# Experts' second layer: two of three row tiles by seven half-width products, accumulated in PSUM

## The chip, the core and the metric

The kernel runs on one core of one Trainium2 chip. The metric is the device time of one execution in microseconds (us); lower is better. A core has five engines that each run their own instructions in order and wait for each other through semaphores: TensorE (PE; its weight loads are listed apart as PEld), VectorE (DVE), ScalarE (ACT), GpSimd (POOL) and SyncE (SP, which only starts transfers here). PE takes its operands from SBUF and writes its sums into PSUM[...]; DVE and ACT read them from there.

## The reference, cut

An attention block (a gated linear recurrence with matrix memory) makes one row of 320 numbers for each of 3072 tokens. Then each token goes through one of 8 experts, chosen by a hash of its id:

```python
N, D, E, F = (3072, 320, 8, 1024)
# w1: (E, D, F), w2: (E, F, D), all float32
expert_idx = token_ids * np.int64(2654435761) % np.int64(E)
for e in range(E):
    mask = expert_idx == e
    xe = x[mask]
    h = np.maximum(xe @ w1[e], 0.0)
    out[mask] = h @ w2[e]
```

The change touches only `h @ w2[e]`.

## The kernel before

The attention block takes the first part of the run and stores the rows of x in memory. The experts follow, one after the other. Each handles 3 tiles of 128 of its tokens and up to 32 more (CAP = 416 columns); the remainders of four experts at a time share one tile (`rest`), and a loop at the end, empty for these inputs, takes what is still left over. `h` is kept transposed: for each of the FB = 8 blocks of F, 128 partitions of F by 416 tokens, so that a slice of it is the stationary operand (lhsT) of the second layer and a block of w2, 128 by 320, the moving one (rhs). [...] two banks of `tp`, four of `mh`, two of `zp`. The pool `xp` keeps two buffers of a tile unless `bufs` says otherwise.

```python
    def scatter(zp, idx, apart):
        zo = xp.tile([P, Dm], F32, name="zo", bufs=4)
        nc.scalar.copy(zo[:], zp[:])
        ins = nc.gpsimd.indirect_dma_start(
            out=out[:, :], out_offset=bass.IndirectOffsetOnAxis(ap=idx, axis=0),
            in_=zo[:], in_offset=None, bounds_check=N - 1, oob_is_err=False,
        )
        ins = getattr(ins, "ins", ins)
        if apart:
            tc.declare_no_dep(ins, group="rows_out", reason="disjoint rows")
            tc.add_to_no_dep_group("rows_out", ins)

# ... turn(): transposes of the rows into xT (PE), a 64-column pad copy on DVE, and the eviction of tp ...

    def layer1(w, xT, h, cols, between=lambda fp: None):

        w1t, w1c, _ = w
        for fp in range(FB // 2):
            hp = [mps.tile([P, CAP], F32, name="mh", bufs=4) for _ in range(2)]

            def halves(first):
                for i in range(2):
                    r = slice(i * P // 2, (i + 1) * P // 2)
                    nc.tensor.matmul(
                        hp[i][:, :cols], lhsT=w1c[r, fp, :], rhs=xT[r, 2, :cols], start=first, stop=not first,
                    )

            def whole(i, first):
                fb = 2 * fp + i
                for db in range(2):
                    nc.tensor.matmul(
                        hp[i][:, :cols], lhsT=w1t[:, db, fb * P : (fb + 1) * P], rhs=xT[:, db, :cols],
                        start=(first and db == 0), stop=(not first and db == 1),
                    )

            def out(i):
                if i == 0:
                    nc.vector.tensor_relu(h[:, 2 * fp, :cols], hp[i][:, :cols])
                else:
                    nc.scalar.activation(h[:, 2 * fp + 1, :cols], hp[i][:, :cols], AF.Relu)

            if fp % 2 == 0:
                for i in range(2):
                    whole(i, True)
                between(fp)
                halves(False)
                for i in range(2):
                    out(i)
            else:
                halves(True)
                for i in range(2):
                    whole(i, False)
                    out(i)
                between(fp)

    def layer2(w, h, n, idx, apart, between=lambda j: None):
        for j in range(n):
            zp = mps.tile([P, Dm], F32, name="zp")
            for fb in range(FB):
                nc.tensor.matmul(
                    zp[:], lhsT=h[:, fb, j * P : (j + 1) * P], rhs=w[2][:, fb, :],
                    start=(fb == 0), stop=(fb == FB - 1),
                )
            scatter(zp, idx(j), apart)
            between(j)

```

The loop over the experts; `fetch` gathers the rows of an expert on the GpSimd queue, `turns` gives the four pieces of work that transpose the next expert's rows, and layer 1 calls one of them in each of its four steps:

```python
# ...
        def rest(g):
            zp = mps.tile([P, Dm], F32, name="zp")
            for fb in range(FB):
                for i in range(EG):
                    nc.tensor.matmul(
                        zp[i * RM : (i + 1) * RM, :], lhsT=hrem[g][:, i, fb, :], rhs=W[g * EG + i][2][:, fb, :],
                        start=(fb == 0), stop=(fb == FB - 1),
                    )
            scatter(zp, cols_of(s_idx, NR + g)(0), True)

# ...
        for e in range(E):
            g, i = e // EG, e % EG
            if e + 2 < E:
                fetch(e + 2)
            h = xp.tile([P, FB, CAP], F32, name="h")
            if i == 0:
                hrem[g] = xp.tile([P, EG, FB, RM], F32, name="hrem")
            ahead = turns(e + 1) if e + 1 < E else []

            def one(_):
                if ahead:
                    ahead.pop(0)()
                for _ in range(3):
                    if third:
                        third.pop(0)(nc.scalar)

            def after(j):
                one(j)
                if j == 0 and i == EG - 1:
                    rest(g)

            layer1(W[e], xTs[e], h, CAP, one)
            nc.gpsimd.tensor_copy(hrem[g][:, i], h[:, :, NM:])
            layer2(W[e], h, NJ, cols_of(s_idx, e * NJ), True, after)
            if e + 3 < E:
                load_weights(e + 3)

```

Of the kernel before, what the change touches and what calls it, by code (L numbers as in the profile page):

```python
# [8 lines left out]
F32 = mybir.dt.float32  # L9
# [5 lines left out]
ALU = mybir.AluOpType  # L15
PSUM = bass.MemoryType.PSUM

P = 128
# [4 lines left out]
def kernel(  # L23
# [24 lines left out]
    nc = tc.nc  # L48
# [4 lines left out]
    Dm = H * D  # L53
    E, _, F = moe_w1.shape
    FB = F // P
# [10 lines left out]
    NJ = 3  # L66
# [17 lines left out]
    s_idx = consts.tile([P, NC], I32, name="s_idx")  # L84
    xe = consts.tile([1, NX + 1], I32, name="xe")

    def weights(src1, src2, wpool, w2pool):

        w1t = wpool.tile([P, 2, F], F32, name="w1t")
        w1c = wpool.tile([P, FB // 2, P], F32, name="w1c")  # L90
        w2t = w2pool.tile([P, FB, Dm], F32, name="w2t")
        s1 = src1[: 2 * P, :].rearrange("(a p) f -> p a f", p=P)
        last = src1[2 * P :, :].rearrange("d (a two f) -> two d a f", two=2, f=P)
        s2 = src2.rearrange("(a p) d -> p a d", p=P)
        parts = [
            (t[:, db, f0 : f0 + F // 2], s1[:, db, f0 : f0 + F // 2])
            for t in (w1t,) for db in range(2) for f0 in (0, F // 2)
        ]
        parts += [(w1c[i * P // 2 : (i + 1) * P // 2], last[i]) for i in range(2)]
        parts += [(w2t[:, fb : fb + 2, :], s2[:, fb : fb + 2, :]) for fb in range(0, FB, 2)]  # L100
        return (w1t, w1c, w2t), [lambda eng=nc.sync, d=d, r=r: eng.dma_start(d, r) for d, r in parts]

    W = {}

    def weight_slices(e):

        W[e], slices = weights(moe_w1[e], moe_w2[e], wpools[e % 3 // 2], w2pools[2 <= e < 6])
        return slices

    def load_weights(e):  # L110
        for piece in weight_slices(e):
            piece()
# [4 lines left out]
    with tc.tile_pool(name="gates", bufs=1) as gp, \  # L117
# [476 lines left out]
        def route_table(i):  # L594
            oh_r, oh_c = oh.pop(i)
            tk = ps.tile([P, 2, NC], F32, name="tk", tag="tr", bufs=4)
            for t in range(TH):
                nc.tensor.matmul(tk[:], lhsT=oh_r[:, t, :], rhs=oh_c[:, t], start=(t == 0), stop=(t == TH - 1))
            if i == 0:
                nc.vector.tensor_copy(tv[:], tk[:, 0, :])  # L600
            else:
                nc.vector.tensor_tensor(tv[:], tv[:], tk[:, 0, :], op=ALU.add)
            nc.vector.tensor_tensor(tv[:], tv[:], tk[:, 1, :], op=ALU.add)
# [17 lines left out]
        after = {4: [route_counts], **{13 + i: [lambda i=i: route_table(i)] for i in range(NT // TH)}}  # L621
# [110 lines left out]
        for s in range(NT):  # L732
            b, c = s // NB, s % NB
# [63 lines left out]
    xp = ctx.enter_context(tc.tile_pool(name="xp", bufs=2))  # L797
    mps = ctx.enter_context(tc.tile_pool(name="mps", bufs=2, space=PSUM))

    def gather(xg, idx):  # L800
        nc.gpsimd.indirect_dma_start(  # L801
            out=xg, out_offset=None, in_=x_d[:, :], in_offset=bass.IndirectOffsetOnAxis(ap=idx, axis=0),
        )

    def scatter(zp, idx, apart):
        zo = xp.tile([P, Dm], F32, name="zo", bufs=4)
        nc.scalar.copy(zo[:], zp[:])  # L807
        ins = nc.gpsimd.indirect_dma_start(  # L808
            out=out[:, :], out_offset=bass.IndirectOffsetOnAxis(ap=idx, axis=0),
            in_=zo[:], in_offset=None, bounds_check=N - 1, oob_is_err=False,  # L810
# [6 lines that stand above are left out]
    def turn(xg, dst, on_act):  # L817

        tp = mps.tile([P, DB, P], F32, name="tp")
        for db in range(2):  # L820
            nc.tensor.transpose(tp[:, db, :], xg[:, db * P : (db + 1) * P], ident[:])
        nc.vector.tensor_copy(xg[:, Dm:], xg[:, 2 * P : Dm])
        nc.tensor.transpose(tp[:, 2, :], xg[:, 2 * P :], ident[:])  # L823
        if on_act:
            nc.scalar.copy(dst, tp[:])
        else:
            nc.vector.tensor_copy(dst, tp[:])  # L827
        return tp
# [42 lines left out]
# [8 lines that stand above are left out]
            scatter(zp, idx(j), apart)  # L879
            between(j)  # L880

    def cols_of(t, c0):
        return lambda j: t[:, c0 + j : c0 + j + 1]

    with tc.manual_schedule():
        xgs, xTs, remT, hrem = {}, {}, {}, {}

        def fetch(e):
            if e % EG == 0:
                xgs[-1 - e // EG] = xp.tile([P, DB * P], F32, name="xr")  # L890
            xgs[e] = xp.tile([P, NJ, DB * P], F32, name="xg", bufs=3)
            for j in range(NJ):
                gather(xgs[e][:, j, :Dm], cols_of(g_idx, e * NJ)(j))
            if e % EG == 0:
                gather(xgs[-1 - e // EG][:, :Dm], cols_of(g_idx, NR + e // EG)(0))

        def turns(e):
            xT = xTs[e] = xp.tile([P, DB, CAP], F32, name="xT")

            def tile_of(j):  # L900
                turn(xgs[e][:, j, :], xT[:, :, j * P : (j + 1) * P], j % 2 == 1)

            def remainder():
                i = e % EG
                if i == 0:
                    remT[e // EG] = xp.tile([P, DB, P], F32, name="remT")
                    tp = turn(xgs[-1 - e // EG], remT[e // EG][:], True)
                if e == 0:
                    nc.vector.tensor_copy(xT[:, :, NM:], tp[:, :, :RM])  # L909
                    return  # L910
                nc.gpsimd.tensor_copy(xT[:, :, NM:], remT[e // EG][:, :, i * RM : (i + 1) * RM])

            return [lambda j=j: tile_of(j) for j in range(NJ)] + [remainder]
# [11 lines that stand above are left out]
        fetch(0)  # L925
        fetch(1)

        third = weight_slices(2)

        idle = mps.tile([P, CAP], F32, name="mh", bufs=4)  # L930

        def spin(n):
            for _ in range(n):
                nc.tensor.matmul(idle[:], lhsT=ident[:], rhs=W[0][0][:, 0, :CAP], start=True, stop=True)

        spin(11)
        for piece in turns(0):
            piece()
            spin(1)
        for e in range(E):  # L940
            g, i = e // EG, e % EG
            if e + 2 < E:
                fetch(e + 2)
            h = xp.tile([P, FB, CAP], F32, name="h")
            if i == 0:
                hrem[g] = xp.tile([P, EG, FB, RM], F32, name="hrem")
# [13 lines that stand above are left out]

            layer1(W[e], xTs[e], h, CAP, one)
            nc.gpsimd.tensor_copy(hrem[g][:, i], h[:, :, NM:])  # L962
            layer2(W[e], h, NJ, cols_of(s_idx, e * NJ), True, after)
            if e + 3 < E:
                load_weights(e + 3)

    nx = nc.values_load(xe[0:1, NX : NX + 1], min_val=0, max_val=NX)
    with tc.If(nx > 0):
        with tc.For_i(0, nx, 1) as k:
# [4 lines left out]
            w, slices = weights(  # L974
                moe_w1[bass.ds(ex, 1)].rearrange("e d f -> (e d) f"),
                moe_w2[bass.ds(ex, 1)].rearrange("e f d -> (e f) d"), wpools[0], w2pools[0],
            )
# [4 lines left out]
            h = xp.tile([P, FB, CAP], F32, name="h")  # L982
# [34 lines left out]
```

## Time and profile before

| | |
|---|---|
| time, median of 3 runs | 424.4 us (424.22 to 425.66) |
| span of the profiled execution | 424.8 us |
| PE busy | 390.1 us (92%) |
| PEld busy | 258.9 us (61%) |
| DVE / ACT / POOL busy | 138.6 / 134.4 / 120.3 us |
| second layer (line L875), PE busy | 105.2 us |
| first layer (lines L846 and L839), PE busy | 96.2 and 26.7 us |

The profile is one execution, recorded by the hardware. "Busy" is the time in which an engine has an instruction in work. A row of a group reads: line, engine, operation, what is written <- what is read, shapes, count | busy us, mean ns of one | us that the engine sat idle before such instructions, and what ended the wait. A row of the timeline reads: start us, length us, engine, line, operation, operands, count, and in brackets the idle time before it with its releaser. Each fp32 product of the program is two MATMUL instructions in the records, and matmuls are pipelined: the next starts before the listed end of the one before, so their mean duration is longer than their spacing. L807 is ACT's copy of zp to zo, L808 the scatter to the output, L822 and L827 (or L825 on ACT) the pad copy and the eviction of `turn`, L853 and L855 the relus, L388, L436, L441, L336 and L368 sums and products of the attention block.

### The profile page before, as it was taken

To read this page: it belongs to the slowest core of one execution; us is meant where nothing else is said; L and a number is where in the kernel's file an instruction comes from. 1 tells how busy PE (TensorE), PEld (TensorE's weight loads), DVE (VectorE), ACT (ScalarE), POOL (GpSimd) and SP (SyncE) were. 2 spreads that over 40 slices of the span, in tenths; PEclk is the share of its full clock that TensorE was granted. 3 is DMA by queue.
4 is the path that set the end of the run, shared out by engine and by line. 5 is a ranking of instruction groups with operands and counts; after the bars stand their busy time and mean duration, and the time that the engine had idled before them with its cause. 6 is when DMAs were issued, how large, how long until landed. Compare 5 with 4: busy or idle time off the path is not lost.

```text
span 424.8 us, 7425 instructions
## 1 busy us (share of the span) xinstructions
PE 390.1 (92%) x2868; PEld 258.9 (61%) x2868; DVE 138.6 (33%) x384; ACT 134.4 (32%) x238; POOL 120.3 (28%) x210
## 2 busy tenths in 40 slices
PE   2467999999999997999999999999999999999992
PEld 1356877877777774556657556556556566575551
DVE  6454657767776862221120110110110201201100
ACT  5256786596586471011111011110101111111010
POOL 6264313322544520711312501312302312020021
PEclk9988999999999999999999999999999999999998
DMA  8929889889776731457518217245126200000000
GB/s 158 226 59 166 183 189 194 183 202 207 188 159 149 165 99 42 120 179 235 178 31 262 83 57 234 63 121 164 60 86 194 62 15 31 0 16 32 0 17 30
DMA packets 111784, 51.37 MB, mean 121 GB/s; under 512 B 86624, under 2 KB 105892, under 8 KB 111748
## 3 DMA queue, kind: packets, MB, share of 16 engines
q1 hardware_dynamic: 105898, 39.31, 38.8%
q0 software_dynamic: 2496, 8.20, 6.0%
q10 hardware_dynamic: 3354, 3.37, 2.5%
q8 instruction: 23, 0.38, 0.4%
q14 instruction: 13, 0.11, 0.1%
HBM read 42.00 MB, written 8.63 MB: 119 GB/s over the span
## 4 chain that ended last, share of the span: by engine, by line
PE 77%; ACT 6%; issue 5%; DMA 4%; POOL 3%; DVE 2%; SPq 1%; ACTq 1%; POOLq 0%; DVEq 0%
PE mh L846 22%; PE zp L875 21%; PE sp L351 6%; PE mh L839 6%; PE ht L409 5%; PE ht L402 3%; PE ab L311 2%; PE tr L275 2%; PE xo L424 2%; PE ht L382 2%; ACT hT L417 1%; DMA R<-decay_pieces 1%; ACT qT L289 1%; PE tr L288 1%; PE xb L323 1%
## 5 line engine op out<-in xcount | busy, mean ns | idle before, releaser
L875 PE MATMUL zp<-w2t,h 128*128 128x320 f32 x384 | 105.2, 433 | 0.0
L846 PE MATMUL mh<-xT,w1t 128*128 128x416 f32 x256 | 96.2, 519 | 0.2 <-DVE xT L909 0.2
L875 PEld LDWEIGHTS zp<-w2t,h 128*128 128x128 f32 x384 | 72.7, 190 | 32.0 <-issue 3.3
L846 PEld LDWEIGHTS mh<-xT,w1t 128*128 128x128 f32 x256 | 46.7, 190 | 42.4 <-issue 40.4
L827 DVE COPY xT<-tp 128x384 f32<-128x384 f32 x16 | 8.9, 557 | 138.4 <-PE tp L823 96.1
L808 POOL DMA_INDIRECT out_dram<-zo,s_idx x26 | 25.6, 985 | 92.6 <-ACT zo L807 92.6
L855 ACT ACTIVATE h<-mh 128x416 f32<-128x416 f32 x32 | 16.5, 517 | 107.4 <-PE mh L839 58.8
L807 ACT COPY zo<-zp 128x320 f32<-128x320 f32 x26 | 11.1, 425 | 101.1 <-PE zp L875 92.9
L853 DVE TENSOR_SCALAR h<-mh 128x416 f32<-128x416 f32 x32 | 18.9, 591 | 53.5 <-PE mh L839 27.5
L359 DVE TENSOR_TENSOR w<-sp,w 128x512 f32<-128x512 f32 x48 | 30.9, 686 | 13.4 <-PE sp L351 10.0
L351 PE MATMUL sp<-qT,kT 64*128 64x128 f32 x384 | 30.6, 304 | 4.0 <-ACT qT L289 4.0
L441 POOL TENSOR_TENSOR x<-x,den 128x320 f32<-128x320 f32 x23 | 16.6, 722 | 57.6 <-DVE den L439 27.8
L351 PEld LDWEIGHTS sp<-qT,kT 64*128 64x128 f32 x384 | 25.7, 204 | 10.7 <-ACT qT L289 5.8
L315 ACT ACTIVATE w<-ab 128x512 f32<-128x512 f32 x48 | 26.6, 610 | 6.0 <-PE ab L311 5.9
L801 POOL DMA_INDIRECT xg<-x_rows,g_idx x24 | 23.3, 973 | 13.5 <-issue 13.5
L839 PE MATMUL mh<-xT,w1c 64*128 64x416 f32 x128 | 26.7, 535 | 0.0
L409 PE MATMUL ht<-w,v 128*64 128x128 f32 x384 | 26.7, 282 | 0.0
L962 POOL COPY hrem<-h 128x256 f32<-128x256 f32 x8 | 3.2, 397 | 81.4 <-ACT h L855 81.4
L417 ACT COPY hT<-ht 128x512 f32<-128x512 f32 x24 | 14.1, 586 | 33.5 <-PE ht L409 30.8
L409 PEld LDWEIGHTS ht<-w,v 128*64 128x64 f32 x384 | 20.9, 139 | 4.2 <-issue 3.3
L289 ACT COPY qT<-tr 128x512 f32<-128x512 f32 x24 | 22.8, 974 | 0.6 <-PE tr L288 0.3
L311 PE MATMUL ab<-R,L 128*64 128x512 bf16 x96 | 16.8, 409 | 5.9 <-DMA L<-input_pieces 2.6
(185 smaller groups left out, 420.2 us busy)
## 6 DMA issues: line engine op xcount, KB each, us to landing
w2t<-in_moe_w_dram SPq DMA_DIRECT2D x28, 320.0 KB
w1t<-in_moe_w_dram SPq DMA_DIRECT2D x28, 256.0 KB
k<-in_k_dram SPq DMA_DIRECT2D x24, 160.0 KB
v<-in_v_dram SPq DMA_DIRECT2D x24, 160.0 KB
og<-in_o_gate_dram SPq DMA_DIRECT2D x24, 160.0 KB
x_rows<-x SPq DMA_DIRECT2D x24, 160.0 KB
ql<-in_q_dram SPq DMA_DIRECT2D x6, 480.0 KB
w1c<-in_moe_w_dram SPq DMA_DIRECT2D x14, 128.0 KB
```

Source lines behind the costliest of these rows:

```text
L289: nc.scalar.copy(qb[b]["T"][:, :, cols], tp[:])
L311: nc.tensor.matmul(ab[i * HB : (i + 1) * HB], lhsT=Ls[b % 2][:, c * P + i * HB : c * P + (i + 1) * HB], rhs=R[:, i, hf::2, :], start=True, ...
L315: nc.scalar.activation(w[:, hf], ab[:], AF.Exp)
L351: nc.tensor.matmul(sp[hf][:, j, :], lhsT=d["kT"][r, j, :], rhs=q_of(s)[r, j, :], start=True, stop=True,)
L359: nc.vector.tensor_tensor(d["w"][:, hf], d["sp"][hf][:], d["w"][:, hf], op=ALU.mult)
L409: nc.tensor.matmul(place(j, hf), lhsT=d["v"][:, 2 * j + hf, :], rhs=d["w"][:, hf, j, :], start=(c == 0 and j0 == 0), stop=True, skip_group ...
L801: nc.gpsimd.indirect_dma_start(out=xg, out_offset=None, in_=x_d[:, :], in_offset=bass.IndirectOffsetOnAxis(ap=idx, axis=0),)
L808: ins = nc.gpsimd.indirect_dma_start(out=out[:, :], out_offset=bass.IndirectOffsetOnAxis(ap=idx, axis=0), in_=zo[:], in_offset=None, bound ...
L839: nc.tensor.matmul(hp[i][:, :cols], lhsT=w1c[r, fp, :], rhs=xT[r, 2, :cols], start=first, stop=not first,)
L846: nc.tensor.matmul(hp[i][:, :cols], lhsT=w1t[:, db, fb * P : (fb + 1) * P], rhs=xT[:, db, :cols], start=(first and db == 0), stop=(not fir ...
L853: nc.vector.tensor_relu(h[:, 2 * fp, :cols], hp[i][:, :cols])
L875: nc.tensor.matmul(zp[:], lhsT=h[:, fb, j * P : (j + 1) * P], rhs=w[2][:, fb, :], start=(fb == 0), stop=(fb == FB - 1),)
```

## The change

Tile 2 of an expert is still done by eight full-width products. Tiles 0 and 1 are done together, as a 2 by 2 block product by seven half-size products (Winograd's form of Strassen's method) in place of eight. The blocks are: A_jk, tile j of h over the even (k = 0) or odd (k = 1) blocks of F, and B_kc, the same blocks of w2 in the left (c = 0) or right (c = 1) 160 columns. With

- s1 = A10 + A11, s2 = s1 - A00, s3 = A00 - A10, s4 = A01 - s2 (on DVE, 128x512 each)
- t1 = B01 - B00, t2 = B11 - t1, t3 = B11 - B01, t4 = B10 - t2 (on GpSimd, 128x640 each)

the seven products are A00 B00, s2 t2, A01 B10, s3 t3, s1 t1, A11 t4 and s4 B11. Each is four accumulated products (128 by 128 by 160) of the program. They go into the halves of two zp tiles, ya and yb of one, xa and xb of the other; some sums are left to PSUM by going on with a half that has been read meanwhile (ya gets A01 B10 on top of A00 B00; xa and xb likewise), the rest is done on DVE while the halves are evicted. The purpose is to have PE stream fewer columns: seven eighths of those of tiles 0 and 1.

The whole diff but for its headers:

```diff
@@ -805,6 +805,9 @@
     def scatter(zp, idx, apart):
         zo = xp.tile([P, Dm], F32, name="zo", bufs=4)
         nc.scalar.copy(zo[:], zp[:])
+        send(zo, idx, apart)
+
+    def send(zo, idx, apart):
         ins = nc.gpsimd.indirect_dma_start(
             out=out[:, :], out_offset=bass.IndirectOffsetOnAxis(ap=idx, axis=0),
             in_=zo[:], in_offset=None, bounds_check=N - 1, oob_is_err=False,
@@ -879,6 +882,70 @@
             scatter(zp, idx(j), apart)
             between(j)
 
+    DH = Dm // 2
+
+    def sums_of_w2(w2t):
+
+        b = [[w2t[:, k::2, c * DH : (c + 1) * DH] for c in range(2)] for k in range(2)]
+        t1, t2, t3, t4 = (xp.tile([P, FB // 2, DH], F32, name=f"t{i}", bufs=1) for i in range(1, 5))
+        for d, x, y in ((t1, b[0][1], b[0][0]), (t2, b[1][1], t1), (t3, b[1][1], b[0][1]), (t4, b[1][0], t2)):
+            nc.gpsimd.tensor_tensor(d[:], x, y[:] if y in (t1, t2) else y, op=ALU.subtract)
+        return t1, t2, t3, t4
+
+    def layer2_pair(w, sums, h, idx, between):
+
+        w2t = w[2]
+        t1, t2, t3, t4 = sums
+        a = [[h[:, k::2, j * P : (j + 1) * P] for k in range(2)] for j in range(2)]
+        s1, s2, s3, s4 = (xp.tile([P, FB // 2, P], F32, name=f"s{i}", bufs=1) for i in range(1, 5))
+        nc.vector.tensor_tensor(s1[:], a[1][0], a[1][1], op=ALU.add)
+        nc.vector.tensor_tensor(s2[:], s1[:], a[0][0], op=ALU.subtract)
+        nc.vector.tensor_tensor(s3[:], a[0][0], a[1][0], op=ALU.subtract)
+        nc.vector.tensor_tensor(s4[:], a[0][1], s2[:], op=ALU.subtract)
+
+        zp = mps.tile([P, Dm], F32, name="zp")
+        for fb in range(FB):
+            nc.tensor.matmul(
+                zp[:], lhsT=h[:, fb, 2 * P : 3 * P], rhs=w2t[:, fb, :], start=(fb == 0), stop=(fb == FB - 1),
+            )
+        scatter(zp, idx(2), True)
+        between(0)
+
+
+        def product(dst, x, y, start):
+            for i in range(FB // 2):
+                nc.tensor.matmul(
+                    dst, lhsT=x[:, i], rhs=y[:, i], start=(start and i == 0), stop=(i == FB // 2 - 1),
+                    skip_group_check=True,
+                )
+
+        def half(k, c):
+            return w2t[:, k::2, c * DH : (c + 1) * DH]
+
+        z0, z1 = (xp.tile([P, Dm], F32, name="zo", bufs=4) for _ in range(2))
+        p1, u2, u3 = (xp.tile([P, DH], F32, name=name, bufs=1) for name in ("p1", "u2", "u3"))
+        y = mps.tile([P, Dm], F32, name="zp")
+        x = mps.tile([P, Dm], F32, name="zp")
+        ya, yb, xa, xb = y[:, :DH], y[:, DH:], x[:, :DH], x[:, DH:]
+        product(ya, a[0][0], half(0, 0), True)
+        nc.scalar.copy(p1[:], ya)
+        product(yb, s2, t2, False)
+        nc.vector.tensor_tensor(u2[:], yb, p1[:], op=ALU.add)
+        product(ya, a[0][1], half(1, 0), False)
+        nc.scalar.copy(z0[:, :DH], ya)
+        between(1)
+        product(xa, s3, t3, True)
+        nc.vector.tensor_tensor(u3[:], xa, u2[:], op=ALU.add)
+        product(xb, s1, t1, False)
+        nc.vector.tensor_tensor(z1[:, DH:], xb, u3[:], op=ALU.add)
+        product(xa, a[1][1], t4, False)
+        nc.vector.tensor_tensor(z1[:, :DH], xa, u2[:], op=ALU.add)
+        send(z1, idx(1), True)
+        product(xb, s4, half(1, 1), False)
+        nc.vector.tensor_tensor(z0[:, DH:], xb, u2[:], op=ALU.add)
+        send(z0, idx(0), True)
+        between(2)
+
     def cols_of(t, c0):
         return lambda j: t[:, c0 + j : c0 + j + 1]
 
@@ -941,6 +1008,7 @@
             g, i = e // EG, e % EG
             if e + 2 < E:
                 fetch(e + 2)
+            sums = sums_of_w2(W[e][2])
             h = xp.tile([P, FB, CAP], F32, name="h")
             if i == 0:
                 hrem[g] = xp.tile([P, EG, FB, RM], F32, name="hrem")
@@ -960,7 +1028,7 @@
 
             layer1(W[e], xTs[e], h, CAP, one)
             nc.gpsimd.tensor_copy(hrem[g][:, i], h[:, :, NM:])
-            layer2(W[e], h, NJ, cols_of(s_idx, e * NJ), True, after)
+            layer2_pair(W[e], sums, h, cols_of(s_idx, e * NJ), after)
             if e + 3 < E:
                 load_weights(e + 3)
```

## The prediction

> **What bounds the kernel now.** I read the page's shares first, then the stretch in which the changed lines run, then one expert in order of time, then single lines for durations. TensorE (PE) is busy 92% of the span; what matters is the experts' stretch alone, so I asked for the busy time of each engine between the first layer-1 product and the end of the last layer-2 product (columns: window, length, then busy time and count of PE, PEld, DVE, ACT, POOL, clock, DMA share and GB/s):
>
> ```profile
> 178.80:417.10 238.30, 238.24 (x962) 142.78 (x962) 29.02 (x68) 30.13 (x65) 48.05 (x59) 1.00 0.31 96
> ```
>
> PE is idle for 0.06 of 238.3 us, at full clock. Nothing else is near a limit: whatever PE does not do is gained, and whatever it waits for is lost, one to one. The groups of the page say what a product costs, and the timeline shows one expert's layer 2 (from 314.30) with its evictions:
>
> ```profile
> L875 PE MATMUL zp<-w2t,h 128*128 128x320 f32 x384 | 105.2, 433 | 0.0
> ...
> L846 PE MATMUL mh<-xT,w1t 128*128 128x416 f32 x256 | 96.2, 519 | 0.2 <-DVE xT L909 0.2
> ```
> ```profile
> 306.26 0.38 PE L821 MATMUL tp<-ident,xg 128*128 128x128 f32 x2
> 306.48 0.27 PE L823 MATMUL tp<-ident,xg 128*128 128x128 f32 x1
> 306.58 2.96 PE L846 MATMUL mh<-xT,w1t 128*128 128x416 f32 x8
> ...
> 314.30 13.08 PE L875 MATMUL zp<-w2t,h 128*128 128x320 f32 x48
> ...
> 318.80 0.42 ACT L807 COPY zo<-zp 128x320 f32<-128x320 f32 x1 [3.79 <-PE zp L875]
> ```
>
> The program's 3 x 8 products of an expert are 48 instructions here: an fp32 product is issued twice. The spacing of starts, not the listed duration, is the cost. For 320 columns it is (13.08 - 0.43)/47 = 0.269 us; for 416, (2.96 - 0.52)/7 = 0.349; for 128, (0.38 - 0.27)/1 = 0.11. The differences give (0.349 - 0.269)/96 = 0.83 ns a column. The evictions (ACT zo) hide because the next tile is accumulated in the other zp buffer.
>
> [...] An exposed load in the trace costs 105 (below); a hidden one fits the 0.10 us between L823 at 306.48 and L846 at 306.58. [...] The trace shows two engines that only read one bank kept apart: DVE L909 starts when ACT's read of the same tp ends (178.46), though it reads the same columns and changes nothing. [...] L822's copy takes 184 ns at the median, and the one at 243.26 that met a GpSimd copy took 309.
>
> ```profile
> 177.98 0.48 ACT L825 COPY remT<-tp 128x384 f32<-128x384 f32 x1 [1.91 <-issue]
> 178.49 0.26 DVE L909 COPY xT<-tp 128x96 f32<-128x96 f32 x1 [0.93 <-issue]
> ...
> 178.80 0.30 PEld L846 LDWEIGHTS mh<-xT,w1t 128*128 128x128 f32 x2 [0.83 <-DVE xT L909]
> 178.80 3.06 PE L846 MATMUL mh<-xT,w1t 128*128 128x416 f32 x8 [0.16 <-DVE xT L909]
> ```
>
> **Part 1: fewer columns.** Per expert, tiles 0 and 1 now take 2 x 8 x 2 = 32 instructions of 320 columns: 32 x 0.269 = 8.61 us. After: 7 products x 4 blocks x 2 = 56 instructions of 160 columns, each 0.269 - 160 x 0.833/1000 = 0.136 us (the weight load of 0.105 still hides under it): 56 x 0.136 = 7.62. Saved: 0.99 us an expert, 7.9 us in all. That is the whole possible gain, 1.9%.
>
> **Part 2: waits between products.** Four accumulators lie in two PSUM tiles: ya, yb are halves of one bank, xa, xb of the other. In the built program (its order and its semaphores, no time in it) each product into a bank waits for the eviction of the other half of that bank, not only of its own half: the product s2*t2 into yb waits for ACT's copy p1 of ya; h*w2 into ya waits for DVE's u2, which reads yb; s1*t1 into xb waits for u3 (reads xa); h*t4 into xa waits for the first z1 sum (reads xb); s4*w2 into xb waits for the second z1 sum (reads xa). Only the step from y to x, the first product and the return to layer 1 are free. So at five places an expert PE runs dry: product, eviction, product, with nothing between.
>
> One such place, counted from the start of the product's last instruction:
> - its end: 0.165 + 0.133 = 0.298 us (the listed duration is 433 at 320 columns and 519 at 416, some 165 above the 0.833 a column);
> - PE's end to the eviction's start: 0.04 to 0.10 (zo: last PE instruction ended at 318.77, copy began at 318.80);
> - the eviction of 128x160: DVE 0.325, from a sum of the same kind with one PSUM operand at 128x164; ACT 0.29, from L807's 425 at 320 and L825's 473 at 384, so 0.84 ns a column below 320;
> - back to PE: 0.05 (L909 ends 178.75, PE begins 178.80), some 0.07 more where a separate wait instruction stands before the product (two of the five);
> - the first weight load, no longer hidden: 0.105. That first L846 in the fence shows it: its eight instructions span 3.06 us where eight that follow without a wait span 2.96.
> - less the slot that would have passed anyway: 0.136.
>
> ```profile
> L388 DVE TENSOR_TENSOR C<-C,ht 128x164 f32<-128x164 f32 x16 | 5.2, 325 | 5.2 <-PE ht L382 4.2 <-POOL x L441 0.8
> ```
>
> With a hand-over of 0.10 for the two evictions that have two semaphores (p1, u2) and 0.05 for the rest: p1 0.298 + 0.10 + 0.29 + 0.12 + 0.105 - 0.136 = 0.78; u2 0.74; u3 0.69; first z1 0.76; second z1 0.69. Sum 3.67 us an expert.
>
> **Part 3: what lies beside.** DVE makes s1 to s4 (128x512, 0.69 us each: L436's 487 ns at 320 columns plus 192 at the 1.04 ns a column between it and L388; so 2.8): they start when the last relu of h ends, 0.7 us into layer 2, and end at about 3.5; s2 is first needed at 4.35 + 1.09 = 5.4, since tile 2's eight products go first. Hidden. GpSimd makes t1 to t4 (128x640, two inputs; 721 ns at 320 columns and 460 at 164 give 1.26 us each, 5.0 an expert). GpSimd reaches them after the last scatter and the gathers (these end 5.8 us into the expert that starts at 327.22) and ends at 10.8; t2 is needed near 21 (layer 2 begins at 15.7). Hidden, and GpSimd has idle time (48 of 238 us busy). But they lie where DVE copies L822 for the next expert's transposes (7.0 us into an expert, needed 0.6 us later): blocked up to one GpSimd sum of 1.26 us, some PE wait of 0 to 0.6. I put 1 us for all seven such experts. ACT loses two 320-column copies (0.85) and gains two of 160 (0.58); neither counts. The tail after the last product (scatter, 7.7 us) is the same within 0.1.
>
> **Sum.** 424.4 + 8 x (3.67 - 0.99) + 1 = 424.4 + 21.4 + 1 = 446.8; I say 446.5 us, 5% slower.
>
> **The rivals.**
> (a) The saving stands and the waits are hidden: 424.4 - 7.9 = 416.5. For it: PE is the bound and loses columns, everything added lies on engines that are 80% idle. Against it: the waits stand in the built program, and PE takes its products in program order, so nothing fills the gap. To hide the waits, the products into y and x would have to alternate; here they follow each other bank by bank.
> (b) Weight loads become the bound at 160 columns: if a load and its hand-over took the listed 190 ns rather than 105, 56 x 0.19 = 10.6 us an expert, 2.0 more than now, or 16 us over all, and the waits on top: about 463. Against it: 128-column passes run at 0.11 with a new weight each.
> (c) GpSimd or DVE is late with t2 or s2, so that PE waits before the second product too. It would need GpSimd sums of over 3.5 us each in place of 1.26. Unlikely; it would cost several us an expert: 460 and more.
> (d) The gaps lower PE's clock. About 60% of the second half of layer 2 stays busy; in the attention stage stretches of 3.4 us with PE 53 to 66% busy (155 to 165 us) kept the full clock, and the two that fell to half followed stretches with 5 and 35%. If it fell for one stretch of 3.4 us an expert, 8 x 1 to 1.7 = 8 to 14 us more: 455 to 460.
>
> **Range and chances.** The gain (7.9) is known to 0.5 us. The wait is five times some 0.73 us; an error of 0.1 in each is 4 us over all, upward more than down (clock, GpSimd). So 441 to 453. To be within 2%, under 432.9, the five waits would have to come to 2.0 us an expert, 0.4 each, less than the eviction and the weight load alone with the product's own end. I give 0.95 to slower, 0.03 to within, 0.02 to faster.
>
> **What would show it.** In the changed profile: 448 instructions of 160 columns with spacing 0.136 inside a product; 40 idle stretches of PE before them of about 0.4 to 0.5 us (the weight load hides in a longer first instruction, about 0.40 in place of 0.30), released by ACT p1 (8) and DVE u2, u3, zo (32); none by GpSimd's t. An expert, 28.7 us from one layer 2 (314.30) to the next (342.96), becomes about 31.4. Wrong it would be if PE went on writing one half of a bank while the other is read, if the 160-column spacing were not 0.136, or if the idle stretches named GpSimd.

## The result, and the profile after

| kernel | median us | range, runs | ratio to before, 95% interval |
|---|---|---|---|
| before | 425.03 | 424.22 to 427.02, 4 | 1 |
| changed | 447.68 | 447.45 to 448.27, 4 | 1.0528 (1.0487 to 1.0568) |

The changed kernel is 5.3% slower, 22.7 us by the medians. Nearly all of that lies between the first layer-1 product and the last layer-2 product. The busy time of each engine there, in the changed kernel (same columns as the window of before):

```profile
176.90:437.70 260.80, 241.16 (x1154) 156.07 (x1154) 70.60 (x139) 28.75 (x66) 100.67 (x91) 1.00 0.28 87
```

The stretch is 260.8 us long where it was 238.3, and PE, which had 0.06 us of idle time in it, now has 19.6 (260.80 - 241.16). The granted clock is 1.00 throughout. (In this profile the experts begin 1.9 us earlier, at 176.9 in place of 178.8; the attention stage is the same code in both, and its end moves by that much between profiles.) The groups of the second layer in the page of the changed kernel, L908 for tile 2 and L917 for the seven products (two of its four rows), show where the idle time sits:

```profile
L917 PE MATMUL zp<-t,s 128*128 128x160 f32 x192 | 31.5, 307 | 7.1 <-DVE u L938 3.3
L908 PE MATMUL zp<-w2t,h 128*128 128x320 f32 x128 | 35.8, 432 | 0.0
...
L917 PE MATMUL zp<-w2t,h 128*128 128x160 f32 x128 | 21.0, 307 | 3.9 <-DVE u L933 3.9
```

The full-width products of tile 2 wait for nothing; those of 160 columns do. What PE waited for, over the whole run of the changed kernel (columns: who, for whom, us in total, times, longest us):

```profile
PE zp L917 <- DVE u L933: 3.9, 8, 0.5
PE zp L917 <- DVE zo L940: 3.9, 8, 0.5
...
PE zp L917 <- DVE u L938: 3.3, 8, 0.4
PE zp L917 <- DVE zo L942: 3.3, 8, 0.4
...
PE zp L917 <- issue: 2.8, 6, 0.5
PE tp L826 <- DVE xg L825: 1.5, 2, 1.0
...
PE zp L917 <- ACT p L931: 0.9, 2, 0.4
```

Five waits for each of eight experts: u2 (L933), u3 (L938), the two sums into z1 (L940, L942) and the copy p1 (L931). Six of the eight waits for p1 are listed under "issue": there the profile names no releaser, but in the timeline below the copy p1 ends at 329.72 and PE goes on at 329.82. None names a sum on GpSimd (t) or a sum of h (s). One expert in order of time shows the alternation, with PE, DVE and ACT taking turns:

```profile
323.78 4.47 PE L908 MATMUL zp<-w2t,h 128*128 128x320 f32 x16
...
328.09 1.25 PE L917 MATMUL zp<-w2t,h 128*128 128x160 f32 x8
...
329.43 0.29 ACT L931 COPY p<-zp 128x160 f32<-128x160 f32 x1 [0.72 <-PE zp L917]
329.82 1.33 PE L917 MATMUL zp<-t,s 128*128 128x160 f32 x8 [0.48 <-issue]
331.25 0.32 DVE L933 TENSOR_TENSOR u<-zp,p 128x160 f32<-128x160 f32 x1 [4.03 <-PE zp L917]
331.63 1.35 PE L917 MATMUL zp<-w2t,h 128*128 128x160 f32 x8 [0.49 <-DVE u L933]
332.82 1.25 PE L917 MATMUL zp<-t,s 128*128 128x160 f32 x8
...
334.11 0.33 DVE L938 TENSOR_TENSOR u<-zp,u 128x160 f32<-128x160 f32 x1 [2.53 <-PE zp L917]
334.49 1.35 PE L917 MATMUL zp<-t,s 128*128 128x160 f32 x8 [0.42 <-DVE u L938]
...
336.35 1.32 PE L917 MATMUL zp<-t,h 128*128 128x160 f32 x8 [0.51 <-DVE zo L940]
...
338.10 1.35 PE L917 MATMUL zp<-w2t,s 128*128 128x160 f32 x8 [0.42 <-DVE zo L942]
...
339.29 2.96 PE L849 MATMUL mh<-xT,w1t 128*128 128x416 f32 x8
```

From 328.09 to 339.29 the seven products take 11.20 us. Their 56 instructions have a spacing of 0.136 us inside a product (start to start in the records; the row of eight gives it too, (1.25 - 0.30)/7), which makes 7.62. The other 3.58 are the five waits. Besides the first product, the step at 332.82, from the y bank to the x bank, is the only one without a bracket. One wait in pieces, that for u3: the product at 332.82 ends at 334.07, DVE reads it from 334.11 to 334.44, and PE goes on at 334.49.

### The profile page after: what moved, and what is told of

It reads as the page before. It is cut to its first block, busy times and chain, and to the rows that moved or that the text cites. A ratio compares the mean times of both kernels' runs of the same rounds, so it can differ in the third digit from the quotient of the medians.

```text
span 445.9 us, 7987 instructions
## 1 busy us (share of the span) xinstructions
PE 391.2 (88%) x3060; PEld 270.9 (61%) x3060; DVE 179.9 (40%) x456; ACT 132.6 (30%) x238; POOL 173.3 (39%) x242
## 5 line engine op out<-in xcount | busy, mean ns | idle before, releaser
L917 PE MATMUL zp<-t,s 128*128 128x160 f32 x192 | 31.5, 307 | 7.1 <-DVE u L938 3.3
L908 PE MATMUL zp<-w2t,h 128*128 128x320 f32 x128 | 35.8, 432 | 0.0
L351 PE MATMUL sp<-qT,kT 64*128 64x128 f32 x384 | 29.7, 297 | 4.3 <-ACT qT L289 4.3
L917 PEld LDWEIGHTS zp<-t,s 128*128 128x128 f32 x192 | 26.9, 190 | 10.7 <-DVE u L938 5.3
L908 PEld LDWEIGHTS zp<-w2t,h 128*128 128x128 f32 x128 | 24.3, 190 | 11.1 <-issue 2.2
L892 POOL TENSOR_TENSOR t<-w2t,t 128x640 f32<-128x640 f32 x16 | 24.6, 1540 | 0.6
L892 POOL TENSOR_TENSOR t<-w2t 128x640 f32<-128x640 f32 x16 | 24.8, 1547 | 0.1
L917 PE MATMUL zp<-w2t,h 128*128 128x160 f32 x128 | 21.0, 307 | 3.9 <-DVE u L933 3.9
```

The source lines that it names most:

```text
L351: nc.tensor.matmul(sp[hf][:, j, :], lhsT=d["kT"][r, j, :], rhs=q_of(s)[r, j, :], start=True, stop=True,)
L892: nc.gpsimd.tensor_tensor(d[:], x, y[:] if y in (t1, t2) else y, op=ALU.subtract)
L908: nc.tensor.matmul(zp[:], lhsT=h[:, fb, 2 * P : 3 * P], rhs=w2t[:, fb, :], start=(fb == 0), stop=(fb == FB - 1),)
L917: nc.tensor.matmul(dst, lhsT=x[:, i], rhs=y[:, i], start=(start and i == 0), stop=(i == FB // 2 - 1), skip_group_check=True,)
```

## The experiments

Times are medians with the interval of the ratio to the kernel before on the same chip (there 424.24 us for the first four, 424.70 for the last two). The theory is that the waits by PSUM bank make the loss. What is called a bank is the PSUM buffer of one tile; no trace here shows more of it than that. Its rivals are the side work (sums on GpSimd and DVE), weight loads at 160 columns, and waits for data rather than for a bank. Beside the time of the whole run, each result gives one length from the records, called the stretch from here on, which leaves the attention block out: from the start of the first layer-1 product to the start of the last layer-2 product. It is 237.8 us before and 260.5 us in the changed kernel.

**Four banks.** Same products in the same order; each accumulator in a bank of its own.

```diff
-        y = mps.tile([P, Dm], F32, name="zp")
-        x = mps.tile([P, Dm], F32, name="zp")
-        ya, yb, xa, xb = y[:, :DH], y[:, DH:], x[:, :DH], x[:, DH:]
+        ya, yb, xa, xb = (mps.tile([P, CAP], F32, name="mh", bufs=4)[:, :DH] for _ in range(4))
...
-        product(yb, s2, t2, False)
+        product(yb, s2, t2, True)
...
-        product(xb, s1, t1, False)
+        product(xb, s1, t1, True)
```

> The changed kernel with the same seven products in the same order, but the four accumulators ya, yb, xa, xb in four PSUM banks (the buffers of mh, free in layer 2) in place of two halves of two banks. Theory of the waits by bank: all five waits (28.5 us over the eight experts in the changed kernel's records) go, since each eviction now lies beside the next product: 447.7 - 28.5 = 419 us, about 6 us under the kernel before. Rival, the sums on GpSimd and DVE slow PE or the weight loads do: nothing changes, 446 to 448 us.

Measured 419.74 us, ratio 0.9886 (0.9838 to 0.9933): 28 us under the changed kernel and 1.1% (4.5 us; some 6 were expected) under the kernel before. The stretch is 232.0 us, 28.5 less than in the changed kernel. The busy times of the experts (same columns as above), and the same part of one expert, its PE rows and two evictions (in this kernel L929 is the copy p1, L931 u2):

```profile
177.40:409.80 232.40, 230.84 (x1154) 154.98 (x1154) 70.03 (x140) 28.79 (x66) 99.06 (x90) 1.00 0.31 97
```

```profile
314.41 1.25 PE L917 MATMUL mh<-w2t,h 128*128 128x160 f32 x8
...
315.50 1.25 PE L917 MATMUL mh<-t,s 128*128 128x160 f32 x8
315.70 0.29 ACT L929 COPY p<-mh 128x160 f32<-128x160 f32 x1 [0.66 <-PE mh L917]
316.59 1.25 PE L917 MATMUL mh<-w2t,h 128*128 128x160 f32 x8
316.86 0.33 DVE L931 TENSOR_TENSOR u<-mh,p 128x160 f32<-128x160 f32 x1 [3.30 <-PE mh L917]
317.67 2.34 PE L917 MATMUL mh<-t,s 128*128 128x160 f32 x16
...
319.85 1.25 PE L917 MATMUL mh<-t,h 128*128 128x160 f32 x8
...
320.93 1.25 PE L917 MATMUL mh<-w2t,s 128*128 128x160 f32 x8
...
322.02 2.96 PE L849 MATMUL mh<-xT,w1t 128*128 128x416 f32 x8
```

No bracket on any PE row: 7.61 us for the seven products, the 7.62 of the columns alone. The evictions are as long as before and run while the next product does. All the data dependences are still there (u3 still needs u2, for instance), so PE had not been waiting for data.

**Two products exchanged.** The smallest edit that hides some of the waits and not others:

```diff
+        product(xa, s3, t3, True)
         product(ya, a[0][1], half(1, 0), False)
         nc.scalar.copy(z0[:, :DH], ya)
         between(1)
-        product(xa, s3, t3, True)
```

> The changed kernel with only the third and the fourth product exchanged, so that a product into the x bank lies between two into the y bank. Theory of the waits by bank: the waits for u2 (0.755 us) and for u3 (0.685) are hidden, the other three stay: 8 x 1.44 = 11.5 us less, 436 us. Rival, PE waits for the data of the sums (s, t, u) and not for the bank: the order doesn't matter, 447 to 448 us.

Measured 437.42 us, ratio 1.0291 (1.0236 to 1.0346), 10.3 us less than the changed kernel; expected were 11.5, and the stretch is 249.0 us, 11.5 less. The waits view of this run, in the experts' stretch, has lost exactly the rows of u2 and u3:

```profile
PE zp L917 <- DVE zo L940: 3.9, 8, 0.5
PE zp L917 <- DVE zo L942: 3.3, 8, 0.4
PE zp L917 <- issue: 2.8, 6, 0.5
PE tp L826 <- DVE xg L825: 1.5, 2, 1.0
PE zp L917 <- ACT p L931: 0.9, 2, 0.4
```

**The side work alone.** The kernel before with the sums t1 to t4 (GpSimd) and s1 to s4 (DVE) made for each expert and read by nothing.

```diff
... sums_of_w2 as in the changed kernel; sums_of_h, its four sums of h ...
+            sums_of_w2(W[e][2])
             h = xp.tile([P, FB, CAP], F32, name="h")
...
+            sums_of_h(h)
             layer2(W[e], h, NJ, cols_of(s_idx, e * NJ), True, after)
```

> The kernel before with the four sums of w2 on GpSimd and the four sums of h on DVE added for each expert, and nothing that reads them: the side work alone. Theory of the waits by bank: PE never waits for the sums; only the pad copies that meet a GpSimd sum delay a few transposes, 1 to 3 us in all, 426 to 428 us. Rival, the side work is the cause: 440 us or more.

Measured 426.75 us, ratio 1.0053 (1.0026 to 1.0080): 2.5 us, far from the 22.7 of the change. In its records PE waits 1.1 us in all, at two places, for pad copies (L822), and at no place for a sum; the stretch is 1.2 us longer than before. The interval of the ratio, 1.1 to 3.4 us, reaches down to that; the rest of the 2.5 us is not placed.

**Half-width products alone.** The kernel before with tiles 0 and 1 each made as a left and then a right half of 160 columns, so eight blocks twice; tile 2 and the remainders stay at full width.

```diff
-            for fb in range(FB):
-                nc.tensor.matmul(
-                    zp[:], lhsT=h[:, fb, j * P : (j + 1) * P], rhs=w[2][:, fb, :],
+            for cs in [slice(0, DH), slice(DH, Dm)] if apart and j < 2 else [slice(0, Dm)]:
+                for fb in range(FB):
+                    nc.tensor.matmul(
+                        zp[:, cs], lhsT=h[:, fb, j * P : (j + 1) * P], rhs=w[2][:, fb, cs],
...
```

> The kernel before with tiles 0 and 1 of each expert by half-width products, the left half of zp and then the right, eight blocks each: twice as many instructions of 160 columns with a new weight for each, no sums, no new eviction. Theory: 512 x 0.136 in place of 256 x 0.269 us, 0.8 us more, 425 to 426.5 us. Rival, weight loads bound at 160 columns: each 0.19 us, 28 us more, 453 us.

Measured 425.06 us, ratio 1.0028 (1.0003 to 1.0053): 0.8 us, as foretold from 0.003 us for each pair of halves (2 x 0.136 - 0.269); the stretch is 0.6 us longer. With a new weight for every 160 columns that is all it costs here, so weight loads are out as a cause.

**Pad copies moved.** Four banks left three places where PE waited for a 64-column pad copy of the next expert's rows (1.15, 0.16 and 0.64 us over the usual spacing; the view below lists the two longer ones). On top of the four banks, one DVE instruction at the start of an expert makes the next expert's three copies, before GpSimd begins its sums.

```diff
... the copy in turn() is left out, but for the first expert ...
+            if e + 1 < E:
+                nc.vector.tensor_copy(xgs[e + 1][:, :, Dm:], xgs[e + 1][:, :, 2 * P : Dm])
             sums = sums_of_w2(W[e][2])
```

> The kernel with four banks, and the pad copies of the next expert's rows made in one DVE instruction at the start of an expert, ahead of the GpSimd sums, in place of three between the transposes. Theory: the 1.9 us that PE waits for pad copies held up by GpSimd sums (three places in the profile with four banks) go, 419.7 - 1.9 = about 418 us, 0.984 to 0.986 of the kernel before. Rival, the pad copies were late for another reason (DVE's own queue): 419 to 420 us and the waits stay.

Measured 417.37 us, ratio 0.9854 (0.9805 to 0.9904). The interval overlaps that of four banks without it, so the time alone doesn't show the 1.9 us; the records do: the stretch is 229.9 us, 2.1 less than with four banks alone, and 7.9 less than before the change. The waits of PE in the experts' stretch, four banks first, then with the copies moved:

```profile
PE tp L826 <- DVE xg L825: 1.5, 2, 1.0
PE mh L849 <- DVE xT L974: 0.2, 1, 0.2
```
```profile
PE mh L850 <- DVE xT L975: 0.2, 1, 0.2
```

**Alternating banks.** The two zp banks are kept; only the order changes, with one more ACT copy each of the first xa and xb sums, so that their banks come free early.

```diff
+        product(xa, s3, t3, True)
+        nc.scalar.copy(p4[:], xa)
         product(ya, a[0][0], half(0, 0), True)
         nc.scalar.copy(p1[:], ya)
+        product(xb, s1, t1, False)
+        nc.scalar.copy(z1[:, DH:], xb)
         product(yb, s2, t2, False)
         nc.vector.tensor_tensor(u2[:], yb, p1[:], op=ALU.add)
-        product(ya, a[0][1], half(1, 0), False)
-        nc.scalar.copy(z0[:, :DH], ya)
+        nc.vector.tensor_tensor(u3[:], p4[:], u2[:], op=ALU.add)
+        nc.vector.tensor_tensor(z1[:, DH:], z1[:, DH:], u3[:], op=ALU.add)
         between(1)
-        product(xa, s3, t3, True)
-        nc.vector.tensor_tensor(u3[:], xa, u2[:], op=ALU.add)
-        product(xb, s1, t1, False)
-        nc.vector.tensor_tensor(z1[:, DH:], xb, u3[:], op=ALU.add)
         product(xa, a[1][1], t4, False)
         nc.vector.tensor_tensor(z1[:, :DH], xa, u2[:], op=ALU.add)
         send(z1, idx(1), True)
+        product(ya, a[0][1], half(1, 0), False)
+        nc.scalar.copy(z0[:, :DH], ya)
```

> The changed kernel with its two zp banks kept, but the seven products in the order xa, ya, xb, yb, xa, ya, xb, and one more ACT copy each of the first xa and xb sums, so that every eviction lies beside a product into the other bank. Theory of the waits by bank: all five waits go without more PSUM, as with four banks: 418 to 421 us. Rival, four banks helped for another reason than the missing waits (where the sums lie, or the mh buffers): near 440 us or more.

Measured 417.84 us, ratio 0.9850 (0.9814 to 0.9886); the stretch is 231.8 us. The five waits are gone here as well, with the sums in the two banks where they were:

```profile
PE tp L826 <- DVE xg L825: 1.5, 2, 1.0
PE mh L849 <- DVE xT L978: 0.2, 1, 0.2
```

So it is the wait, not the place. The last two kernels are both some 1.5% faster than the kernel before; between them the runs make no difference. Two things stay open. In these kernels every PSUM tile counts as a bank of its own, so no run tells a wait by bank from a wait by tile. And the waits stand in the program, as semaphores: letting PE write one half of a bank while the other half is read was not tried, so no run shows what would happen without them.

## Why the prediction was right

The prediction said 446.5 us (441 to 453); 447.68 was measured. Step by step:

**Part 1, fewer columns.** Predicted spacing 0.136 us and a saving of 0.99 us an expert. The spacing is 0.136 in the records, the waitless products of the four-bank kernel take 7.61 us, and the half-width run excludes weight loads (rival b). With the waits and the late pad copies gone, the stretch is 7.9 us shorter than before, which is the saving foretold. (The 463 us given to rival b is a slip of the sum: it adds 16 us to a total that still holds the saving. With 10.6 in place of 7.62 us an expert the sum comes to about 471.)

**Part 2, the waits.** From the start of the last instruction of a product to the second of the next, less two slots of 0.136, median over the experts: p1 0.72 us, u2 0.75, u3 0.69, first z1 0.75, second z1 0.68, together 3.59; predicted were 0.78, 0.74, 0.69, 0.76, 0.69, together 3.67. Over all 28.5 us for 29.4. The forms foretold are there: 40 idle stretches of 0.4 to 0.5 us, evictions of 0.292 on ACT and 0.325 on DVE, hand-overs to the eviction of 0.09 us (p1), 0.11 (u2) and 0.04 (the other three), foretold as 0.10 and 0.05, and back to PE of 0.10 (p1), 0.15 (first z1) and 0.06 (the other three), foretold as 0.12 and 0.05, and a first instruction listed at up to 0.404 us in place of 0.299, where its weight load begins with it (both at 331.63 and 334.49). The expert that took 28.7 us from one layer 2 to the next takes 31.5 (31.4 foretold). With two of the five waits hidden the stretch is 11.5 us shorter, with all five hidden, in two different ways, 28 us and more; that shows them to be the cause. One reading in the working was loose: 425 and 473 ns at 320 and 384 columns give 0.75 ns a column, not 0.84, and so 0.305 us for ACT's eviction, not 0.29; the 0.292 measured at 160 happens to fit the 0.84.

**Part 3, what lies beside.** The sums of h took 0.69, 0.77, 0.68 and 0.68 us and ended 3.45 us into layer 2 (3.5 predicted). A GpSimd sum took 1.54 us where 1.26 was worked out from shorter ones; that term was too small, though t2 was still ready 12 us or more before its use (rival c didn't come). The pad copies cost 1.95 us in place of 1, at three of seven experts and up to 1.14 us at one, above the 0.6 given as the most: the two copies of that row stand for 2.10 us in the timeline where two take 0.29 in the kernel before. All eight pad copies listed at over 0.5 us ended 0.05 to 0.07 us after the end of a GpSimd sum beside them; the other 18 took 0.18 to 0.30 us.

```profile
246.45 2.10 DVE L825 COPY xg<-xg 128x64 f32<-128x64 f32 x2
...
246.83 1.55 POOL L892 TENSOR_TENSOR t<-w2t 128x640 f32<-128x640 f32 x1
...
248.50 0.33 PE L826 MATMUL tp<-ident,xg 128*128 128x128 f32 x1 [0.98 <-DVE xg L825]
```

The clock stayed at 1.00 in the stretch (rival d): in any 3.4 us of it PE was at least 71% busy. The shares that the prediction gives for that rival are lower than the listed durations say: 65 to 78% in the stretches from 155 to 165 us, and 9 and 38% before the two that fell to half. The profile of the changed kernel adds one of 51% (27.14 to 30.55 us), itself at a clock of 0.50, that was followed by another 3.4 us at 0.50.

The tail was foretold as unchanged within 0.1 us. From the end of the last product it takes 8.15 us where it took 7.77, and 8.15 to 8.32 in all runs with the seven products.

**The sum.** -7.9 + 28.5 + 1.95 = 22.5 us. The records give 22.7 for the stretch (237.8 before, 260.5 after), the medians 22.7. The prediction's own sum is 22.4 (-7.9 + 29.4 + 1): that it comes so close is in part luck, since the waits were put 0.9 us too high and the pad copies 0.95 us too low. The mechanism, five waits of the sizes named, does not hang on that. Rival a (416.5) was wrong for this order of products, and right as a statement of what the change is worth: the two mended kernels came to 417.4 and 417.8.

## What to carry to other kernels

Count a PSUM tile as one lock when you plan the order: in the changed kernel all five products of an expert whose accumulator shared a tile with one being evicted waited for that eviction, though their columns are apart. PE was the bound there, and each such step cost it the product's own end (0.30 us), two hand-overs (0.04 to 0.11 and 0.06 to 0.15), the eviction (0.29 to 0.33) and a weight load that no longer hid (0.07 to 0.10), less the usual slot (0.136): 0.68 to 0.75 us for 160 columns. Before splitting a product into smaller ones, list the order of the tiles that they go into, and alternate them or give each accumulator its own. A saving in columns of 1.9% was real all along; the order of seven products, with two more small copies, decided whether it showed as 1.5% faster or 5.3% slower.

## What the runs showed that was not expected

- A GpSimd sum of two SBUF operands at 128x640 took 1.54 us, more than the 1.26 that two shorter ones (0.460 at 164 columns, 0.722 at 320) lead to in a straight line.
- DVE and GpSimd each took longer beside the other. GpSimd's copy of h's remainder took 0.92 us while DVE ran a sum with two SBUF inputs, where it took 0.40 in the kernel before, and the second DVE sum took 0.77 in place of 0.69; at the one expert where GpSimd's copy began only after that sum had started, it took 0.69. A pad copy of 64 columns, 184 ns at the median, was listed at 1994 ns at worst, beside a GpSimd sum of 1553 ns (246.83 us).
